# Two loads issued ahead of a program's opening barrier, in a cached attention decode that reads 570 MB

## The chip, the cores and the metric

The kernel runs on one core of a Trainium2 chip; the other cores are idle. The metric is the time of one execution on the device, in microseconds (us). A profile is one of these executions, recorded; its span runs from the first to the last instruction of the program and is about 2 us shorter than the measured time.

The engines by their short names in the profile: PE is TensorE (PEld its weight loads), DVE is VectorE, ACT is ScalarE, POOL is GpSimd, SP is SyncE, which here does nothing but issue loads and the two final stores. A `q` after a name (SPq, ACTq) means the engine's sequencer, which issues DMAs and waits for semaphores.

## The reference

Two independent attention blocks decode one token each, and their outputs are concatenated. All tensors are bf16.

```python
# A: 32 heads, each with its own cache of 32768 keys and values, head size 128
q = (x @ wq).reshape(B, Sq, H, Dh).transpose(0, 2, 1, 3)          # x: [1, 1, 512]
scores = einsum("bhqd,bhkd->bhqk", q, k_cache) * (Dh ** -0.5)
p = softmax(scores, axis=-1)
o = einsum("bhqk,bhkd->bhqd", p, v_cache)
a = o.transpose(0, 2, 1, 3).reshape(B, Sq, H * Dh) @ wo

# B: 32 query heads on 8 key/value heads, and only the last 4096 keys
k = repeat(k_cache[:, :, Sk - W:, :], rep, axis=1)                # W = 4096, rep = 4
...                                                               # then as A
out = concatenate([a, b], axis=-1)                                # [1, 1, 1024]
```

Block A reads 32 heads x 2 x 8.39 MB of cache. Block B reads 4 loads of 4.19 MB of its small cache. Each block also reads `wq` and `wo`, 4.19 MB each. Nothing is read twice, and every byte passes through the DMA engines.

## The kernel before

The kernel builds one list of operations per engine (`self.prog["sp"]` and so on), works out the semaphores between them, and emits each list in a block of its engine. Opening the block comes after a barrier of all five engines: each engine reports with a drain instruction, and goes on when all have reported.

```python
    def build(self):
        nc = self.nc
        with nc.Block() as block:
            self.alloc()
            self.plan()
            self.sems = {}
            for e in self.engines:
                self.assign(e)
            block.gpsimd(self.emit("pool"))
            block.vector(self.emit("dve"))
            block.scalar(self.emit("act"))
            block.sync(self.emit("sp"))
            block.tensor(self.emit("pe"))
```

All large loads go through SyncE, in the order of the plan. The first four need no wait; each of them is 4.19 MB.

```python
    def load(self, dst, src, sem, *deps):
        self.op("sp", lambda e: e.dma_start(dst, src).then_inc(sem, 16), *deps)
    ...
        self.load_wq("B")          # B's query weights      -> vbuf, first half
        self.load_b("k", 0)        # B's keys, heads 0 to 3 -> kbuf
        self.load_wq("A")          # A's query weights      -> vbuf, second half
        self.load_b("k", 1)        # B's keys, heads 4 to 7 -> kbuf
        self.emit_qproj("B")       # q of B on TensorE: needs wq_B and x_B
        self.emit_unit("B", 0)     # transposes and scores of B's first keys
        self.emit_qproj("A")
        ...
        for g in range(2):
            ...
            self.load_b("v", g)    # waits until TensorE has freed vbuf
        ...
        for g in range(NQH):       # the 32 heads of A
            self.load_k(g, 1 if g < NQH - 1 else 2)   # waits for free key buffers
            self.load_v(g)                            # waits for the free value buffer
```

Of the kernel before, what the change touches and what calls it, by code (L numbers as in the profile page):

```python
# [52 lines left out]
class _Kernel:  # L53
# [37 lines left out]

    def build(self):
        nc = self.nc
        with nc.Block() as block:
            self.alloc()
            self.plan()
            self.sems = {}
            for e in self.engines:
                self.assign(e)
            block.gpsimd(self.emit("pool"))  # L100
            block.vector(self.emit("dve"))
            block.scalar(self.emit("act"))
            block.sync(self.emit("sp"))
            block.tensor(self.emit("pe"))

    def assign(self, eng):


        ops = self.prog[eng]
        pos, last = 0, None  # L110
        for o in ops:
            pos = pos + 1 if o.loop is not None and o.loop == last else 0
            o.pos, last = pos, o.loop
        for c in self.engines:
            for o in self.prog[c]:
                for d in o.deps:
                    if isinstance(d, Op) and d.eng == eng and c not in d.users:
                        d.users.append(c)
        shared = {}
        for o in ops:  # L120
            if o.loop is not None:
                u = shared.setdefault(o.pos, [[], None])
                u[0] += [c for c in o.users if c not in u[0]]
                u[1] = u[1] or o.to
        pending = []
        for o in ops:
            key = shared.get(o.pos) if o.loop is not None else None
            users = key[0] if key else o.users
            to = key[1] if key else o.to
            if to is None:  # L130
                to = next((c for c in users + pending), None)
            if key:
                key[1] = to
            o.to = to
            pending = [c for c in dict.fromkeys(pending + users) if c != to]
        assert not pending, (eng, pending)
        n = {c: 0 for c in self.engines}
        for o in ops:
            o.to = shared[o.pos][1] if o.loop is not None else o.to
            o.before = dict(n)  # L140
            if o.to:
                n[o.to] += 1
# [567 lines left out]
```

## Time and profile before

| | before |
|---|---|
| time | 1329.08 us median of 3 runs (1328.71 to 1329.19), the first three of the five in the result below |
| span of the profile | 1326.9 us |
| moved by DMA | 570.66 MB |
| DMA share and rate from 180 to 1240 us | 1.00, 433 GB/s |
| TensorE, VectorE busy | 73%, 56% |

First the page of the kernel before: the share of time that the DMA engines are busy, in tenths, and what they moved, in 40 slices of the span.

```profile
span 1326.9 us, 28821 instructions
...
DMA  9999999999999999999999999999999999999998
GB/s 393 431 433 436 432 431 435 437 429 433 441 429 433 435 435 431 433 441 429 433 435 435 431 433 441 427 435 435 433 433 433 437 431 435 435 431 435 433 435 341
```

The DMA engines are at least 90% busy in every slice but the last. So, at this rate, there are only three places where time can be had: fewer bytes, the head before the first byte, and the tail after the last. This change aims at the head, which the timeline of the kernel before shows. The columns are start, duration, engine, source line, operation, tiles; in brackets the idle time before and what ended it.

```profile
0.80 0.39 ACTq L424 DMA_DIRECT2D x_B<-in_B_x_dram  x1
0.80 0.20 POOL L406 MEMSET ones<- 128x128 bf16 x1 [0.29 <-POOLq L695]
0.80 0.42 SPq L288 DMA_DIRECT2D vbuf<-in_B_wq_dram  x1
1.22 0.46 ACTq L424 DMA_DIRECT2D x_A<-in_A_x_dram  x1
1.29 0.41 SPq L288 DMA_DIRECT2D kbuf<-in_B_k_cache_dram  x1
1.74 0.51 SPq L288 DMA_DIRECT2D vbuf<-in_A_wq_dram  x1
...
13.24 3.55 PE L453 MATMUL psACC<-x_B,vbuf 128*128 128x1 bf16 x128 [13.24 <-DMA vbuf<-in_B_wq_dram]
...
24.26 6.28 PE L497 MATMUL psT<-ident,kbuf 128*128 128x128 bf16 x64 [7.47 <-DMA kbuf<-in_B_k_cache_dram]
```

SyncE issues its first load at 0.80 us. TensorE waits for the first weights until 13.24 us, works 3.55 us, and waits again 7.47 us for the first keys. The view of waits, of SyncE's queue, says what SyncE did before 0.80 us (total wait, number of times, longest); line 695, which makes the program object, is the call that the barrier's instructions are put down to:

```profile
SPq L695 <- PEq L695: 0.7, 1, 0.7
```

The windows view of the kernel before shows when bytes move. Its columns are the window, its length, the busy time of PE, PEld, DVE, ACT and POOL, the granted TensorE clock, the DMA share and GB/s. DMA bytes are counted to the window in which a transfer starts, so a short window can show over 433 GB/s.

```profile
1.75:2.00 0.25, 0.00 (x0) 0.00 (x0) 0.25 (x2) 0.25 (x1) 0.25 (x2) 1.00 0.04 1
2.00:2.25 0.25, 0.00 (x0) 0.00 (x0) 0.25 (x2) 0.25 (x1) 0.25 (x2) 1.00 2.91 788
...
180.00:1240.00 1060.00, 785.35 (x10822) 550.92 (x10821) 608.02 (x1065) 44.44 (x140) 0.00 (x0) 0.84 1.00 433
```

The large loads begin to move at 2.0 us, 1.2 us after the first issue. Last, three pieces of the chain of waits of the kernel before (start, duration, what), for the rhythm in the middle and for the end:

```profile
83.52 5.69 PE psT L497 x64
...
122.20 5.15 PE psT L497 x64
...
1290.45 33.47 DMA kbuf<-in_A_wo_dram
```

One head of A takes 122.20 - 83.52 = 38.7 us, in which 16.78 MB arrive: 433 GB/s again. The last piece of the output weights lands at 1290.45 + 33.47 = 1323.9 us, about 3 us before the end.

### The profile page before, as it was taken

How to read it: one execution, taken by the hardware profiler on the slowest of the kernel's cores; microseconds unless marked ns; L12 is line 12 of the kernel's file. 1: busy time of each engine (PE TensorE's matmuls, PEld its weight loads, DVE VectorE, ACT ScalarE, POOL GpSimd, SP SyncE). 2: the span in 40 equal slices, each digit the busy share in tenths (PEclk: the TensorE clock that was granted, in tenths of full speed). 3: DMA queues.
4: the chain of work that ended last, by engine and by line, in shares of the span. 5: the costliest groups of instructions: out<-in, count | busy, mean ns of one | idle time of the engine just before them, and what ended most of it. 6: DMA issues, size and time to landing. Idle time of an engine off the chain costs nothing.

```text
span 1326.9 us, 28821 instructions
## 1 busy us (share of the span) xinstructions
PE 963.9 (73%) x13436; PEld 678.1 (51%) x13436; DVE 749.5 (56%) x1345; ACT 54.8 (4%) x167; POOL 2.3 (0%) x17
## 2 busy tenths in 40 slices
PE   3657678777667877766787777678777767877786
PEld 3544445554444555444465544446554444655453
DVE  3645466665456666545666645566664556666473
ACT  0000000000000000000000000000000000000000
POOL 0000000000000000000000000000000000000000
PEclk9877788887788888778888878888887888888798
DMA  9999999999999999999999999999999999999998
GB/s 393 431 433 436 432 431 435 437 429 433 441 429 433 435 435 431 433 441 429 433 435 435 431 433 441 427 435 435 433 433 433 437 431 435 435 431 435 433 435 341
DMA packets 13351, 570.66 MB, mean 430 GB/s; under 512 B 1812, under 2 KB 1816, under 8 KB 2200
## 3 DMA queue, kind: packets, MB, share of 16 engines
q1 hardware_dynamic: 13048, 570.44, 99.6%
q8 instruction: 12, 0.20, 0.1%
q10 hardware_dynamic: 288, 0.00, 0.0%
q14 instruction: 3, 0.02, 0.0%
HBM read 570.43 MB, written 0.00 MB: 430 GB/s over the span
## 4 chain that ended last, share of the span: by engine, by line
DMA 70%; PE 27%; DVE 1%; issue 0%; SPq 0%; ACT 0%
DMA kbuf<-in_A_k_cache_dram 65%; PE psT L497 23%; PE psS L519 4%; DMA kbuf<-in_B_k_cache_dram 3%; DMA kbuf<-in_A_wo_dram 3%; DVE kt L500 1%; PE psACC L599 0%; SPq L288 0%; DVE oc_A L615 0%; ACT psb L547 0%; DVE tr_in L536 0%; PE psPT L571 0%; ACT ptsb L574 0%; PE psPT L661 0%; PE psG L626 0%
## 5 line engine op out<-in xcount | busy, mean ns | idle before, releaser
L500 DVE COPY kt<-psT 128x1024 bf16<-128x1024 bf16 x1056 | 654.8, 683 | 245.3 <-PE psT L497 243.5
L497 PE MATMUL psT<-ident,kbuf 128*128 128x128 bf16 x8448 | 578.7, 234 | 176.7 <-DMA kbuf<-in_A_k_cache_dram 165.0
L497 PEld LDWEIGHTS psT<-ident,kbuf 128*128 128x128 bf16 x8448 | 539.3, 106 | 268.7 <-DMA kbuf<-in_A_k_cache_dram 173.1
L599 PE MATMUL psACC<-vbuf,ptsb 128*4 128x512 bf16 (+1 forms) x2112 | 182.9, 522 | 23.3 <-ACT ptsb L574 21.3
L519 PE MATMUL psS<-kt,qw 128*32 128x512 bf16 x2048 | 157.6, 385 | 15.4 <-DVE kt L500 15.4
L613 DVE TENSOR_SCALAR oc_A<-psACC,hot_A 128x128 f32<-128x128 f32 x32 | 11.2, 350 | 247.7 <-PE psG L626 247.7
L599 PEld LDWEIGHTS psACC<-vbuf,ptsb 128*4 128x4 bf16 (+1 forms) x2112 | 59.0, 110 | 137.8 <-issue 87.6
L547 ACT ACTIVATE psb<-psS,nb_A 128x512 bf16<-128x512 f32 x32 | 22.0, 687 | 1169.8 <-DVE nb_A L546 1169.8
L519 PEld LDWEIGHTS psS<-kt,qw 128*32 128x32 bf16 x2048 | 34.0, 95 | 57.9 <-DVE kt L500 31.3
L626 PE MATMUL psG<-oc_A,hw 128*32 128x128 f32 (+1 forms) x128 | 19.3, 227 | 52.3 <-DVE oc_A L615 52.3
L626 PEld LDWEIGHTS psG<-oc_A,hw 128*32 128x32 f32 x128 | 11.4, 109 | 62.5 <-DVE oc_A L615 55.0
L571 PE MATMUL psPT<-ident,psb 128*128 128x128 bf16 x136 | 18.0, 274 | 34.0 <-ACT psb L547 34.0
L615 DVE SCALAR_TENSOR_TENSOR oc_A<-psACC,hot_A,oc_A 128x128 f32<-128x128 f32 x96 | 33.7, 351 | 3.4
L536 DVE TENSOR_REDUCE tr_in<-psS 128x1 f32<-128x512 f32 x34 | 23.5, 692 | 17.1 <-PE psS L519 17.1
L571 PEld LDWEIGHTS psPT<-ident,psb 128*128 128x128 bf16 x136 | 10.1, 117 | 37.1 <-ACT psb L547 36.7
L540 PE MATMUL psACC<-rows,tr_in 128*1 128x64 f32 x64 | 8.7, 217 | 25.5 <-DVE tr_in L536 25.5
L574 ACT ACTIVATE ptsb<-psPT 128x512 bf16<-128x512 bf16 x34 | 20.3, 597 | 28.3 <-PE psPT L571 28.3
L540 PEld LDWEIGHTS psACC<-rows,tr_in 128*1 128x1 f32 x64 | 2.7, 81 | 35.1 <-DVE tr_in L536 35.1
L544 PE MATMUL psACC<-mr_A,nscale 1*128 1x1 f32 x64 | 12.1, 256 | 9.7 <-DVE mr_A L543 9.7
L544 PEld LDWEIGHTS psACC<-mr_A,nscale 1*128 1x128 f32 x64 | 9.4, 182 | 15.7 <-DVE mr_A L543 15.7
L546 DVE COPY nb_A<-psACC 128x1 f32<-128x1 f32 x32 | 5.1, 158 | 15.0 <-PE psACC L544 15.0
L543 DVE TENSOR_REDUCE mr_A<-psACC 1x1 f32<-1x64 f32 x32 | 6.8, 213 | 11.7 <-PE psACC L540 11.7
(71 smaller groups left out, 75.0 us busy)
## 6 DMA issues: line engine op xcount, KB each, us to landing
kbuf<-in_B_k_cache_dram SPq DMA_DIRECT2D x2, 4096.0 KB, 32.3
vbuf<-in_B_v_cache_dram SPq DMA_DIRECT2D x2, 4096.0 KB, 23.9
kbuf<-in_A_k_cache_dram SPq DMA_DIRECT2D x2, 4096.0 KB, 22.0
vbuf<-in_B_wq_dram SPq DMA_DIRECT2D x1, 4096.0 KB, 12.3
vbuf<-in_A_wq_dram SPq DMA_DIRECT2D x1, 4096.0 KB, 32.2
kbuf<-in_B_wo_dram SPq DMA_DIRECT2D x2, 2048.0 KB, 33.1
kbuf<-in_A_wo_dram SPq DMA_DIRECT2D x1, 1408.0 KB, 28.5
kbuf<-in_A_wo_dram SPq DMA_DIRECT2D x1, 1024.0 KB, 30.8
```

Of the source, the lines that this page charges most:

```text
L497: inst = e.transpose(T[:, 128 * k:128 * k + 128], src[:, DH * k:DH * k + DH], self.ident[:, :])
L500: self.copies.append(self.op("dve", lambda v: v.tensor_copy(KT[:, :], T[:, :]), o, to="pe"))
L519: inst = e.matmul(self.S[32 * c:32 * c + 32, :], lhsT=win, rhs=self.kt[(bb + c // 2) % NKT][:, 512 * (c % 2):512 * (c % 2) + 512], start=b ...
L536: o = dve(lambda v: v.reduce_max(tr["in"][:, 0:1], self.S[:, :], axis=AXX), self.sdone, self.k_pool, to="pe" if name == "A" else None)
L540: o = self.op("pe", lambda e: e.matmul(self.ACC[0:1, 0:64], lhsT=tr["in"][:, 0:1], rhs=self.rows64[:, :], start=True, stop=True, skip_grou ...
L544: o = self.op("pe", lambda e: e.matmul(self.ACC[:, 64:65], lhsT=self.nscale[:, :], rhs=t["mr"][0:1, :], start=True, stop=True, skip_group_ ...
L547: self.sread = self.op("act", lambda s: s.activation(out=self.psb[:, :], in_=self.S[:, :], func=ACTF.Exp, bias=t["nb"][:, k:k + 1], scale= ...
L571: inst = e.transpose(PT[:, 128 * jj:128 * jj + 128], self.psb[:, 128 * jj:128 * jj + 128], self.ident[:, :])
L574: self.ptread = self.op("act", lambda s: s.activation(out=self.ptsb[:, :], in_=PT[:, 0:512], func=ACTF.Copy), self.psread, to="pe")
L599: inst = e.matmul(acc[32 * c:32 * c + rows, 0:512], lhsT=lhsT, rhs=rhs, start=begin, stop=end, tile_position=(0, 32 * c), skip_group_check ...
L615: o = self.op("dve", lambda v, src=src, hot=hot: v.scalar_tensor_tensor(out=oc, in0=src, scalar=hot, in1=oc, op0=ALU.mult, op1=ALU.add), p ...
L626: return self.op("pe", lambda e: e.matmul(self.G[0:32, c0 + c:c0 + c2], lhsT=win, rhs=t["oc"][g % 2][:, c:c2], start=False, stop=True, ski ...
```

## The change

SyncE is to begin its first two loads, B's query weights and B's first keys, ahead of the barrier. They depend on nothing and write buffers that nobody touches before, so they need not wait for the other engines. The new step builds the two instructions outside the block and moves them, in the main instruction list, in front of SyncE's drain, which is SyncE's report to the barrier. For that, the plan has to be made before the block opens.

```diff
     def build(self):
         nc = self.nc
+        self.alloc()
+        self.plan()
+        self.early(2)
+        self.sems = {}
+        for e in self.engines:
+            self.assign(e)
         with nc.Block() as block:
-            self.alloc()
-            self.plan()
-            self.sems = {}
-            for e in self.engines:
-                self.assign(e)
             block.gpsimd(self.emit("pool"))
 ...
+    def early(self, n):
+
+        nc = self.nc
+        main = nc.main_func.blocks[0]
+        old = len(main.instructions)
+        for o in self.prog["sp"][:n]:
+            assert not o.deps and not o.users
+            o.fn(nc.sync)
+        del self.prog["sp"][:n]
+        insts = list(main.instructions)
+        at = next(i for i, x in enumerate(insts) if x.engine == mybir.EngineType.SP and type(x).__name__ == "InstDrain")
+        assert at < old < len(insts)
+        main.instructions = insts[:at] + insts[old:] + insts[at:old]
```

Source lines shift by 15 (L288 becomes L303); otherwise the order of instructions on every engine is unchanged.

## The prediction

> **What bounds the kernel now.** The DMA engines, from first byte to last. The slice view shows DMA at 9 tenths in 39 of 40 slices; the windows view from 180 to 1240 us shows a DMA share of 1.00 and 433 GB/s, at the fabric ceiling of 435 GB/s that the Trainium skill states ("DMA: Bandwidth & Descriptors", Specifications); the trace agrees. 570.66 MB at 433 GB/s is 1318 us of the 1326.9 us span. The chain of waits puts 27% on TensorE, but those are the steps by which a buffer is freed and the next load issued, with another load still queued: cache loads land 26.5 to 27.8 us after issue, while 8.39 MB take 19.4 us, so 7 to 8 us of work stand ahead of each issue.
>
> What is left is head and tail. Head: the timeline shows SyncE's first load issued at 0.80 us, the next ones 0.45 to 0.55 us apart; the windows show the first bulk bytes at 2.0 us. SyncE's waits show 0.7 us in the opening barrier. Tail: the last output weights land near 1324 us, then about 3 us.
>
> **What the change does.** Two DMA issues (0.42 and 0.41 us) move ahead of the barrier. No byte, no other wait changes.
> - The first load should issue at 0.05 to 0.15 us, about 0.7 us earlier. If issue to first byte stays 1.2 us, bytes move from 1.3 us.
> - SyncE reaches the barrier about 0.95 us later, so it opens at 1.2 to 1.4 us instead of 0.75. The other engines start 0.5 us later: constants end at 5.5 instead of 4.96 us, the x loads issue near 1.3 and 1.7 us.
> - The third and fourth loads issue near 1.3 and 1.8 us, far ahead of need (4.19 MB take 9.7 us).
>
> **How much is on the critical path.** The shift of the stream is; the late start of the others is not. The first projection starts when the first weights land (13.21 us now, expected 12.5). It needs x_B, which landed 6.3 us after issue; issued at 1.3 us it lands at 8 to 9 us. Were it as slow as x_A (12.9 us), it would come at 14 us, and the projection (3.6 us) would still end before the first keys land (24.25 now, 23.5 then). So TensorE waits for keys as before, later issues move with it, and 0.7 us is carried to the end because the queue never empties. DMA gets no faster.
>
> **Predicted time:** 1329.08 - 0.7 = 1328.4 us, 0.05% less. The runs before spread over 0.5 us, so the gain is hardly above noise. Range 1327.7 to 1329.1. Chances: faster by over 2% 0.005, within 2% 0.99, slower by over 2% 0.005.
>
> **What would show the steps.** Right: first SyncE issue near 0.1 us, third after 1.2 us; GpSimd's fill of `ones` at 1.2 to 1.4 us instead of 0.80; first projection at 12.5 us; first transposes at 23.5 us; a cache period still 38.7 us (83.52 to 122.20 in the chain); the last output weights 0.7 us earlier. Wrong: a first projection after 13.2 us, or landings not shifted though the issue is.
>
> **What would make it wrong.** (a) The first bytes still move at 2.0 us, because something other than the issue gates them: gain 0. (b) SyncE's drain in the barrier waits for the loads to land: the barrier opens at about 23 us, with a gap in the stream, several us slower. (c) The measured time starts with the first instruction, and the early issue moves that start too: gain 0. (d) Drift between sessions over 0.7 us.

## More of the kernel before

The two vectors `x` are loaded from ScalarE's queue, in 128 rows of 8 bytes each:

```python
        for n in ("B", "A"):
            self.op("act", lambda e, n=n: e.dma_start(
                c[n]["x"][:, :], self.X[n]["x"][0, 0, :].rearrange("(p t) -> p t", t=4)).then_inc(self.xsem[n], 16))
```

## The result, and the profile after

| | before | after |
|---|---|---|
| median | 1329.08 us (1328.71 to 1329.19, 5 runs) | 1328.23 us (1327.97 to 1328.52, 5 runs) |
| span of the profile | 1326.9 us | 1326.3 us |

The ratio is 0.9994, with a 95% interval from 0.9982 to 1.0006. A ratio here is the mean time of one kernel's runs over that of the other's of the same rounds, so it is not quite the ratio of the medians. The medians differ by 0.85 us. The interval of the ratio cannot resolve that. What can is the repetition below: the changed kernel was measured in three separate sessions, 15 runs from 1327.75 to 1328.61 us, and the kernel before in those and one more, 32 runs from 1328.66 to 1329.46 us. The two sets do not overlap. The three differences of medians are 0.85, 0.83 and 0.65 us.

The timeline after, the same lines:

```profile
0.00 0.42 SPq L303 DMA_DIRECT2D vbuf<-in_B_wq_dram  x1
...
0.48 0.42 SPq L303 DMA_DIRECT2D kbuf<-in_B_k_cache_dram  x1
1.30 0.39 ACTq L439 DMA_DIRECT2D x_B<-in_B_x_dram  x1
1.30 0.20 POOL L421 MEMSET ones<- 128x128 bf16 x1 [0.81 <-POOLq L710]
1.31 0.34 SPq L303 DMA_DIRECT2D vbuf<-in_A_wq_dram  x1
...
1.72 0.73 ACTq L439 DMA_DIRECT2D x_A<-in_A_x_dram  x1
...
13.35 3.58 PE L468 MATMUL psACC<-x_B,vbuf 128*128 128x1 bf16 x128 [13.35 <-DMA x_B<-in_B_x_dram]
...
23.86 6.00 PE L512 MATMUL psT<-ident,kbuf 128*128 128x128 bf16 x64 [6.93 <-DMA kbuf<-in_B_k_cache_dram]
```

The first load is issued at 0.00 instead of 0.80 us. GpSimd's fill of `ones`, the first thing it does after the barrier, went from 0.80 to 1.30 us: SyncE now reports to the barrier only after its two issues, and everyone else waits for it. (Its first issue alone costs them next to nothing, as e1 below shows.) The first projection did not start earlier but 0.1 us later, and its wait has another name: it no longer waits for the weights but for the little vector `x_B`. The first keys are used 0.4 us earlier. SyncE's own wait in the barrier, and the windows after:

```profile
SPq L710 <- PEq L710: 0.2, 1, 0.2
```

```profile
0.75:1.00 0.25, 0.00 (x0) 0.00 (x0) 0.00 (x0) 0.00 (x0) 0.00 (x0) 1.00 0.00 0
1.00:1.25 0.25, 0.00 (x0) 0.00 (x0) 0.00 (x0) 0.00 (x0) 0.00 (x0) 1.00 4.34 1180
...
180.00:1240.00 1060.00, 792.69 (x10815) 553.01 (x10812) 608.01 (x1065) 44.40 (x140) 0.00 (x0) 0.82 1.00 433
```

Bytes move from 1.0 instead of 2.0 us (the first large packets start at 1.05 and 2.01 us), and the middle of the program runs at the same 433 GB/s. In the chain after, the rhythm and the end:

```profile
82.79 5.57 PE psT L512 x64
...
121.50 5.01 PE psT L512 x64
...
1289.60 33.67 DMA kbuf<-in_A_wo_dram
```

A head of A still takes 38.7 us. The keys arrive 0.7 us earlier at these two heads; in most of the heads after them the chain of this one profile shows 0.4 to 0.5 us. The last weights land at 1323.27, 0.65 us earlier than before (1323.92).

### The profile page after: what moved, and what is told of

Its sections match the earlier page's. It is cut to its first block, busy times and chain, and to the rows that moved or that the text cites. A ratio compares the mean times of both kernels' runs of the same rounds, so it can differ in the third digit from the quotient of the medians.

```text
span 1326.3 us, 28821 instructions
## 1 busy us (share of the span) xinstructions
PE 972.0 (73%) x13436; PEld 681.1 (51%) x13436; DVE 749.4 (57%) x1345; ACT 54.8 (4%) x167; POOL 2.3 (0%) x17
## 4 chain that ended last, share of the span: by engine, by line
DMA 70%; PE 27%; DVE 1%; issue 0%; SPq 0%; ACT 0%
DMA kbuf<-in_A_k_cache_dram 65%; PE psT L512 23%; PE psS L534 4%; DMA kbuf<-in_B_k_cache_dram 3%; DMA kbuf<-in_A_wo_dram 3%; DVE kt L515 1%; PE psACC L614 0%; SPq L303 0%; DVE oc_A L630 0%; ACT psb L562 0%; DVE tr_in L551 0%; PE psPT L586 0%; ACT ptsb L589 0%; PE psPT L676 0%; PE psG L641 0%
## 5 line engine op out<-in xcount | busy, mean ns | idle before, releaser
L614 PE MATMUL psACC<-vbuf,ptsb 128*4 128x512 bf16 (+1 forms) x2112 | 190.4, 539 | 23.2 <-ACT ptsb L589 21.3
L551 DVE TENSOR_REDUCE tr_in<-psS 128x1 f32<-128x512 f32 x34 | 23.5, 692 | 17.3 <-PE psS L534 17.3
## 6 DMA issues: line engine op xcount, KB each, us to landing
vbuf<-in_B_wq_dram SPq DMA_DIRECT2D x1, 4096.0 KB, 12.4
```

The lines of the kernel that those rows point to most:

```text
L551: o = dve(lambda v: v.reduce_max(tr["in"][:, 0:1], self.S[:, :], axis=AXX), self.sdone, self.k_pool, to="pe" if name == "A" else None)
L614: inst = e.matmul(acc[32 * c:32 * c + rows, 0:512], lhsT=lhsT, rhs=rhs, start=begin, stop=end, tile_position=(0, 32 * c), skip_group_check ...
```

## The experiments

The theory: the program is one unbroken stream of loads. It ends earlier by as much as its first byte moves earlier, whatever the other engines do at the start, as long as the queue of loads never runs empty. The main rivals: the gain is drift; every load moved ahead gives its own part; any load out of the barrier's shadow gains; the later start of the other engines, or the later `x_B`, costs part of the gain.

All times below are medians of 5 runs; "before" is the kernel before in the same rounds (9 runs). All results were correct.

| run | first large load issued | first projection | time | before | difference |
|---|---|---|---|---|---|
| changed kernel, first measurement | 0.00 us | 13.35 us | 1328.23 | 1329.08 (5 runs) | -0.85 |
| after_again | 0.00 | 13.48 | 1328.03 | 1328.86 | -0.83 |
| after_third | 0.00 | 13.36 | 1328.39 | 1329.04 | -0.65 |
| e1_one | 0.00 | 13.68 | 1328.25 | 1328.87 | -0.62 |
| e2_four | 0.00 | 13.77 | 1328.30 | 1328.87 | -0.57 |
| e3_late | 3.00 | 15.41 | 1331.07 | 1328.87 | +2.20 |
| e4_xfirst | 1.41 | 13.62 | 1329.47 | 1328.87 | +0.60 |
| e5_xlate | 0.00 | 20.04 | 1328.39 | 1328.86 | -0.47 |
| e5_again | 0.00 | 19.91 | 1328.31 | 1329.04 | -0.73 |
| e6_xlater | 0.00 | 33.26 | 1332.00 | 1328.86 | +3.14 |
| e7_xrow | 0.00 | 12.71 | 1328.31 | 1328.86 | -0.55 |
| e8_both | 0.00 | 12.53 | 1328.23 | 1329.04 | -0.81 |

In the kernel before, the first large load is issued at 0.80 us and the first projection starts at 13.24 us.

### Is it drift? The changed kernel again

No edit; the changed kernel in two further sessions.

> The changed kernel once more, beside the three runs of this call. Theory: 0.6 to 0.9 us less than before, as in the first measurement. Rival (drift): a difference of another size or sign.

> The changed kernel again, as the base of this call, because the run with late x (first projection at 20.0 us) was 0.36 us slower than it in the last call, which the theory calls noise. Theory: 0.6 to 0.9 us less than before.

Measured: 0.83 and 0.65 us less than before. The ratios are 0.9994 and 0.9995. It is not drift: none of the 15 runs of the changed kernel is as slow as the fastest of the 32 runs before. The three differences also tell how finely one can read here: about 0.2 us between sessions.

### How many loads must be early?

```diff
-        self.early(2)
+        self.early(1)      # e1_one
+        self.early(4)      # e2_four
```

> Only the first load (small cache's query weights) ahead of the barrier. Theory (the stream of loads is shifted by as much as its first byte moves, and the queue never empties): first load issued at 0.0 us, second at about 0.9 us, still 8 us before the first has finished, so the whole gain stays: 0.6 to 0.9 us less than before, the same as with two. Rival (each load moved ahead adds its own part, or the keys' load is the one that matters): about half the gain, 0.3 to 0.5 us.

> All four first loads ahead of the barrier, so it opens at about 2.1 us and every other engine and the x loads start about 1.3 us later than before. Theory: no more gain and no loss, 0.6 to 0.9 us less than before; x_B lands near 14 us, the first projection starts there, the first transposes stay at 23.9 us. Rival (the late start of the other engines costs time): 0.5 us or more worse than with two.

Measured: 0.62 us less with one load, 0.57 us less with four, beside 0.65 to 0.85 us with two. The three cannot be told apart at the 0.2 us that sessions differ by. So the first load alone carries what there is; the rival that predicts half the gain for one load (0.3 to 0.5 us) finds no support. Moving the second load ahead does nothing that its later issue would not do, because the first load keeps the engines busy for some 12 us. And with four, where GpSimd's first fill comes at 2.43 us instead of 0.80, the later start of the other engines costs nothing that shows. This fill, in the timelines of e1 and of e2, also tells what an early issue costs the others:

```profile
0.83 0.20 POOL L421 MEMSET ones<- 128x128 bf16 x1 [0.33 <-POOLq L710]
```

```profile
2.43 0.20 POOL L421 MEMSET ones<- 128x128 bf16 x1 [1.93 <-POOLq L710]
```

With none it came at 0.80 us, with one at 0.83, with two at 1.30, with four at 2.43. SyncE had waited 0.7 us in the barrier anyway, so its first issue, of 0.42 us, cost the others 0.03 us; each further one cost them about 0.5 us.

### The head made longer

The kernel before, with one more small fill at the end of GpSimd's constants, for which the first load waits.

```diff
         self.k_hw = pool(lambda g: g.memset(self.hw[:, :], 0.0))
+        self.k_late = self.op("pool", lambda g: g.memset(self.junk[:, :], 0.0), to="sp")
 ...
-        self.load(..., self.mark("v", i))
+        self.load(..., self.mark("v", i), self.k_late if name == "B" else None)
```

> The kernel before, but the first load waits for one more fill that ends GpSimd's list of constants, so it is issued at about 3.2 us instead of 0.80. Theory: one microsecond of head is one microsecond of time: 2.4 us more than before (1331.5), with every landing 2.4 us later. Rival (the end is set by something beside the stream, and the head is hidden; the gain seen was drift): within 0.5 us of before.

The timeline of this run:

```profile
3.00 0.42 SPq L289 DMA_DIRECT2D vbuf<-in_B_wq_dram  x1
```

Measured: the first load was issued 3.00 - 0.80 = 2.20 us later, and the time grew by 2.20 us. The expectation of 2.4 us was made for an issue at 3.2 us; per microsecond of delay it held. The rival, that the head is hidden, is out.

### The wrong loads ahead of the barrier

The kernel before, but the two loads of `x` go ahead of the barrier on ScalarE, and the large loads stay behind it. The helper `early` takes an engine's name for this.

```diff
-        self.early(2)
+        self.early("act", 2)
```

> The kernel before, but the two small x loads go ahead of the barrier on ScalarE, and the large loads stay behind it. Theory: the barrier opens about 0.5 us later, the large stream begins about 0.5 us later, so the time is 0.3 to 0.6 us more than before, though work was moved ahead of the barrier. Rival (any load moved out of the barrier's shadow gains): 0.3 us or more less than before.

The timeline of this run:

```profile
0.12 0.38 ACTq L439 DMA_DIRECT2D x_B<-in_B_x_dram  x1
...
1.41 0.42 SPq L303 DMA_DIRECT2D vbuf<-in_B_wq_dram  x1
```

Measured: `x_B` was issued 0.68 us earlier than before, and the large load 0.61 us later, because the barrier now waits for ScalarE's two issues. The time grew by 0.60 us. This is the same move with the sign turned round. What counts is not that something runs ahead of the barrier but which load does, and issues put ahead of it can delay what stays behind. Since this run builds its program in the changed order too (the plan before the block), it also shows that the new order of building is not what gained.

### Does the late x cost anything?

In the changed kernel `x_B` had become what the first projection waits for. Two runs make it later still: its load waits until the first weights have landed (e5), or until the first keys have (e6). Two make it earlier.

```diff
-    ...then_inc(self.xsem[n], 16))
+    ...then_inc(self.xsem[n], 16),
+        *([(self.vsem[0], 16)] if n == "B" else []))     # e5: B's weights have landed
+        *([(self.ksem[0], 16)] if n == "B" else []))     # e6: B's first keys have landed
```

> The changed kernel, but the x loads are issued only when the first query weights have landed (12.4 us), so x_B lands at about 24 us and the first projection starts about 11 us later than in the changed kernel. Theory: TensorE is about 5 us late with the small cache's first keys, the load of its first values is issued at about 35 us instead of 30.2, while the four loads ahead of it last until about 43.5 us; the queue does not empty and the time is that of the changed kernel within 0.3 us. Rival (x_B's late landing in the changed kernel took part of the gain; the early compute is critical): 2 to 5 us more than the changed kernel.

> The run with late x loads once more, beside the changed kernel in the same rounds. Theory: within 0.25 us of the changed kernel. Rival: again 0.3 us or more slower.

The dose was smaller than intended: `x_B` took 7.4 us instead of 12, so the projection started at 20.04 us and ended 0.9 us after the first keys had landed (22.7 us in this run). The first transposes began at 23.47 us, no later than in the changed kernel (23.86). The time was 0.36 us more than the changed kernel's, which is over the 0.3 us set beforehand, so the run was repeated: 1328.31 us beside 1328.39 us for the changed kernel in the same rounds. The 0.36 us did not come back. A first projection 6.7 us later still lies within the slack, and costs nothing that these measurements resolve.

> The changed kernel, but the x loads are issued only when the first keys have landed (about 23.5 us), so x_B lands at about 35 us. Theory: now the slack is used up: the small cache's first values are issued at about 45 us, after the four loads ahead have landed (43.5 us); the queue empties and the time grows by 3 to 9 us over the changed kernel, with a slice of lower GB/s between 43 and 70 us. Rival (TensorE's early work never matters): the time of the changed kernel within 0.3 us.

The chain of waits of this run, its first pieces, and then the first keys of A:

```profile
0.48 22.02 DMA kbuf<-in_B_k_cache_dram
22.52 10.69 DMA x_B<-in_B_x_dram
33.21 0.05 issue
33.26 3.57 PE psACC L469 x128
36.83 5.29 PE psT L513 x64
...
63.71 23.07 DMA kbuf<-in_A_k_cache_dram
```

The windows view from 13 to 44 us, of the changed kernel and then of this run:

```profile
13.00:44.00 31.00, 19.35 (x421) 17.05 (x422) 13.60 (x31) 0.78 (x2) 0.00 (x0) 0.92 1.01 424
```

```profile
13.00:44.00 31.00, 10.74 (x225) 10.22 (x226) 5.96 (x11) 1.28 (x1) 0.00 (x0) 1.00 0.94 389
```

The same view from 42 to 43 us, again of the changed kernel and then of this run:

```profile
42.00:43.00 1.00, 0.00 (x0) 0.00 (x0) 0.49 (x3) 0.41 (x1) 0.00 (x0) 0.50 1.02 426
```

```profile
42.00:43.00 1.00, 1.00 (x18) 0.52 (x16) 1.00 (x3) 0.00 (x0) 0.00 (x0) 1.00 0.04 16
```

Measured: 1332.00 us, 3.97 us more than the changed kernel in the same rounds. Here the chain runs through `x_B` and TensorE instead of through the stream. B's first values were issued at 42.50 us instead of 30.23. The last of the four loads ahead of them landed at 43.18 us, but nearly all of their packets had started by 42 us, and the first packet of the values started only at 43.54 us. In between the engines were almost idle: 16 GB/s from 42 to 43 us. So the queue did run empty, and the rate from 13 to 44 us was 389 GB/s instead of 424. It stayed low from 44 to 70 us, at 402 GB/s instead of 434. The first keys of A landed at 63.71 + 23.07 = 86.78 us instead of 82.74, and the 4.0 us were not won back. So the start of the other engines has some slack, but not any amount. A delay of 6.7 us is free and one of 19.9 us is not. The expectation had the queue empty at 43.5 us and the issue at 45; both came some 2 us earlier. From the issue of the values to their first packet it was 1.04 us, so by these numbers an issue must come at least that long before the queue runs out.

The two that make `x_B` earlier. First both kinds of loads ahead of the barrier at once:

```diff
-        self.early(2)
+        self.early("sp", 2)
+        self.early("act", 2)
```

> The two large loads ahead of the barrier on SyncE and, at the same time, the two x loads ahead of it on ScalarE. x_B should land at about 6 us instead of 13.3, since its packets are in the rings before the large ones; the first projection should then start at 12.4 us instead of 13.35. Theory (the stream alone counts): the time of the changed kernel within 0.25 us. Rival (x_B's late landing cost part of the gain): 0.3 us or more less than the changed kernel.

Measured: the time is 0.16 us less than the changed kernel's in the same rounds, within the 0.25 us that the theory allows. So an earlier start of the projection (12.53 us) gives nothing either. But `x_B` did not land at 6 us: issued at 0.12 us, it landed 12.4 us later. The expectation was wrong about what makes a small load slow, and the runs together show what does. This is the profile's line on the landing of `x_B` (issue to landing), first in the kernel before, then in the changed kernel, then in e3, where it is issued 2.2 us ahead of the first large load:

```profile
DMA to landing us min/median/max: 6.3/6.3/6.3
```

```profile
DMA to landing us min/median/max: 12.0/12.0/12.0
```

```profile
DMA to landing us min/median/max: 1.7/1.7/1.7
```

The trace's records of single DMA packets say how. The vector is 128 packets of 8 bytes, eight for each of 16 engines. The first weights are 128 packets of 32 KB, most of them about 1.21 us long, again eight per engine. The Trainium skill ("DMA: Bandwidth & Descriptors", section "Queues, rings and completion order") says that a DMA engine goes round the queues that have work, one packet at a time. The records agree with it: in the changed kernel, from 6 to 11 us, as many 8-byte packets as 32 KB packets start in every half microsecond, to within one. Eight turns behind a 1.21 us packet are 9.7 us (an estimate from these two numbers). In e8 the first packet of `x_B` started at 2.80 us, behind the large one at 1.04 us, and the load landed 9.7 us later. In the changed kernel the first packet started only at 5.26 us, 4.0 us after its issue; about five turns then stood behind 32 KB packets and three behind the keys' 8 KB packets, which are about 0.31 us long, and it landed at 13.30 us. In e5 all the large packets beside `x_B` were such 8 KB packets, and it landed in 7.4 us. In the kernel before, the first packet of `x_B` started at 1.80 us, 0.2 us ahead of the first large one at 2.01 us, and 96 of the 128 packets, six of each eight, had started by 2.44 us, with the first large packets; only the other 32 had to take turns. By these records, that is why a head start of 0.2 us halved the time to 6.3 us. Turns are not the whole delay: in e7, below, `x_B` is a single packet, and it too started only at 5.38 us, 4.1 us after its issue. What sets these 4 us was not tested.

The second: each `x` as one row of 1 KB, which TensorE spreads over the partitions with four matmuls of one row each.

```diff
-    e.dma_start(c[n]["x"][:, :], self.X[n]["x"][0, 0, :].rearrange("(p t) -> p t", t=4))
+    e.dma_start(c[n]["xr"][:, :], self.X[n]["x"][0, :, :])
 ...
+    for tt in range(4):
+        e.matmul(self.S[:, 4 * i + tt:4 * i + tt + 1], lhsT=xr[0:1, tt:512:4], rhs=self.ones[0:1, 0:1], ...)
+    ...                                       # then one copy of VectorE into x
```

> The changed kernel, but each x is loaded as one row of 1 KB in one packet instead of 128 packets of 8 bytes, and TensorE spreads it over the partitions with four small matmuls. Theory that the stream is what counts: its first 13 us ran at 411 GB/s instead of 433, about 0.45 us lost, of which the 256 small packets are a part; the first keys land earlier by up to 0.5 us and the time is 0.1 to 0.5 us less than the changed kernel's. Rival (the small packets run beside the large ones at no cost, the slower start is only the filling of the pipeline): the same time within 0.1 us, though x_B lands at about 3 us and the first projection starts at 12.4 us.

Measured: ScalarE's queue moved 4 packets instead of 288, the window from 4 to 13 us (that is the one of the 411 GB/s) ran at 424 instead of 411 GB/s, and the keys were used at 23.40 instead of 23.86 us. The time was 1328.31 us, 0.28 us more than the changed kernel in the same call and 0.08 us less than its median in the next session. The profile of this run, which was its fastest, kept a lead of 0.4 us over the changed kernel to the last landing; its other four runs had spans of 1326.2 to 1326.4 us, those of the changed kernel, in its first measurement, 1326.1 to 1326.5. So the better head of the stream did not become a better time that can be shown. Whether it is worth 0 or 0.2 us stays open, and so does why a lead seen in one profile is not seen in the median. `x_B` itself did not land at 3 us as expected: the four matmuls that needed it started at 7.01 us.

No run beats the changed kernel by more than the sessions differ.

## Why the prediction was right or wrong

**The time: right.** 1328.4 us was predicted, in a range from 1327.7 to 1329.1, and 1328.23 us was measured. The gain of 0.7 us was measured as 0.85, 0.83 and 0.65 us.

**The mechanism: right, and shown.** "The shift of the stream is" on the critical path. Across the runs where the queue stayed full, the time follows the issue of the first large load: -0.80 us of issue gave -0.55 to -0.85 us of time (e5 once -0.47), +0.61 gave +0.60, and +2.20 gave +2.20. That two of these agree to 0.01 us is luck, since sessions differ by 0.2 us. Counted from the start of the first large packet (2.01 us before, 1.05 after, 2.45 in e4, 4.04 in e3) the moves are -0.96, +0.44 and +2.03 us: the same order, but a less close fit. The DMA rate in the middle did not change (433 GB/s), as predicted.

**The barrier: right.** It was to open at 1.2 to 1.4 us; GpSimd's fill started at 1.30 us. The drain does not wait for the loads to land (point (b)), the early issue gates the first bytes (point (a)), and the measured time does not move its own start along (point (c)).

**The first projection: wrong, without effect.** The step that failed is "issued at 1.3 us it lands at 8 to 9 us". It took the 6.3 us of `x_B` before as the cost of the load. In fact `x_B` landed 12.0 us after its issue, at 13.3 us, and the projection started at 13.35 instead of 12.5 us. The 6.3 us belonged to a load of which 96 of 128 packets had started, from 1.80 us on, before they had to take turns with the large load's; behind a large load the same packets took 12 us. The sign that the prediction had set as "wrong", a first projection after 13.2 us, came true, and the time did not suffer. The prediction's fallback held: it reckoned with a landing at 14 us and found that the projection would still end before the first keys. Runs e5, e5_again and e8 confirm that this is slack: projections from 12.53 to 20.04 us give the same time within 0.2 us, except for the one reading of 0.36 us that did not repeat.

**The first keys: half right.** They were expected at 23.5 us and used at 23.86 us (23.75 in the second profile), 0.4 to 0.5 us earlier than before, not 0.7. The last landing was 0.65 us earlier in one profile and 0.76 in the other (1323.92 against 1323.27 and 1323.16), while in between the keys of A landed only 0.4 to 0.6 us earlier. Single profiles of the same kernel differ by 0.1 us, so the path of these last tenths was not followed further.

## What to carry to other kernels

When the DMA engines are busy from the first slice to the last, as here, the time is the head, plus the bytes, plus the tail, and a load that depends on nothing should be issued before the opening barrier; one such load is enough, and it must be the one that starts the long stream. Issues put ahead of a barrier delay everything behind it by what exceeds the wait that their engine had there: here the first one was nearly free and each further one cost the others about 0.5 us. So find the slack of the other engines first: here a first projection 7 us later was free and one 20 us later was not. A gain of 0.06% is below what a 2% verdict can show; repeat it, and use a run that makes the same cause larger (2.20 us of delay for 2.20 us of time) to show it.

## What the Trainium skill lacked or had wrong

- "DMA: Bandwidth & Descriptors", "Queues, rings and completion order", has the round of the queues packet by packet, but no figure for what it costs a small load. Here 1 KB in 128 packets landed 1.7 us after its issue with the rings empty, 6.3 us when 96 of its packets had started before they had to take turns with a large load's, and 12.0 to 12.4 us behind one with 32 KB packets.
- The same section calls a packet "≈9-17 descriptors typical". In this trace each row was recorded as a packet of its own: 256 data packets for the two `x` loads of 128 rows, and 128 packets of 32 KB for weights of 128 rows; and the two queues took turns by these records, one for one.
- The same page, "Where 436 GB/s comes from", says that for loads from HBM the limit of about 358 GB/s per core binds (though its own measurements of a single core are higher, and beside them it ties about 358 to both cores of an HBM domain streaming). With one core running, 433 GB/s came from HBM for 1060 us, within 0.5% of the 435 GB/s that the page gives for the fabric. The limit of 358, put without that condition, does not hold there.
- The same page, Specifications, states a first-byte latency of about 0.6 us for loads issued from SyncE. It agrees if counted from the end of the issue: the issue at 0.00 us took 0.42 us, and the first packet started at 1.05 us, 0.63 us later. In the kernel before, with `x_B`'s packets on the engines, it was 0.79 us (1.22 to 2.01).
- No page says what the opening barrier inside the program costs (0.7 us of SyncE's wait here) or that loads may be issued ahead of it.
